# A rearranged opening, an identity made by GpSimd, and earlier loads and transposes of k in a fused attention and gated-MLP kernel

## The chip, the cores and the metric

The kernel runs on one core of one Trainium2 chip. The metric is the device time in microseconds (us) from launch to end; the median of three runs of the kernel before is 317.84 us (317.53 to 318.85). Beside these, one execution was recorded by the hardware profiler. Its time is 318.65 us, its span from the first to the last recorded instruction 316.9 us. Durations in this text come from that execution.

The engines are called as the profile calls them: PE (TensorE, matrix multiply; its weight loads are PEld), DVE (VectorE), ACT (ScalarE), POOL (GpSimd) and SP (SyncE, here only a queue that issues DMAs). Each engine works through its own instruction stream in order, and waits on semaphores for the others.

## What is computed

Sliding-window causal attention, followed by a feed-forward block with the gate h cos(h):

```python
# q, k, v: (batch 8, heads 8, seq 576, head_dim 64)
scores = scale * np.matmul(q, k.transpose(0, 1, 3, 2))
rel = pos[:, None] - pos[None, :]
mask = (rel >= 0) & (rel < 64)
scores = np.where(mask, scores, -1000000000.0)
attn = np.exp(scores - np.max(scores, axis=-1, keepdims=True))
attn = attn / (np.sum(attn, axis=-1, keepdims=True) + 1e-09)
attn_out = np.matmul(attn, v)
x = attn_out.transpose(0, 2, 1, 3).reshape(4608, 512)
h = x @ w_in            # 512 x 2048
g = h * np.cos(h)
out = g @ w_out         # 2048 x 512
```

Inputs and output are float32.

## The kernel before

**Tiling.** Tokens of all batches form one row of 4608, cut into nine tiles (`mt`) of 512. A batch has 576 tokens, nine blocks (`j`) of 64, so that batch borders and tile borders drift apart. Heads are taken in four pairs (`p`). A score *unit* is one block of 64 queries of both heads of a pair against its 128 keys, a 128x128 tile. Up to four units make a *group*, which has one PSUM bank. Groups 0 to 7 (written `p.g` in the list, half tile g of pair p) hold the blocks of tile 0; groups 8 to 18 hold the last block of batch 0 and all of batch 1; later ones hold a batch each.

**A group's way.** `g_scores` (PE; for groups 0 to 7 an extra matmul with the identity adds the mask, L267), `g_max` (DVE, L293 or L297), `g_exp` (ACT, L308, one exp for each unit), `g_inv` (DVE, L315), `g_norm` (L322, mostly on POOL), `g_trans` (on PE for the first groups and some others, L331, followed by `g_put`; otherwise a DMA transpose from SP's queue, L334, tile wT), `values` (PE, L349 or L368 for half tiles), `put_x` (copies to xT).

**The feed-forward part.** For a tile, 16 groups of matmuls with w_in (L418, or L382 in half tiles) each fill a bank; ACT makes the sine (cos(h) as sin(h + pi/2)), DVE multiplies (L543, or L394 in half tiles), which frees the bank. Then 64 matmuls with w_out (L551, or L401 for tile 0), and a copy to `out_sb`, of which there are two buffers; `store` sends each from SP's queue (L433). ACT's exp and sine use different function tables, and a change of table costs a load.

**Loads.** POOL's queue issues all loads: `load_heads` (q and k of batches 0 and 1, one head pair at a time, L162), `load_chunk` (later batches, six chunks of 96 tokens, L169), `load_v` (five chunks, L175), the four parts of w_in and of w_out (L191, L194). `spread_v` (L180 to L188) makes a copy of v shifted by a half block; for batches from 3 on it is two copies on POOL. q is transposed on PE. k is transposed on PE for batches 0 and 1, and from batch 2 on by six DMA transposes from SP's queue (`turn_k`, L239), into one of two buffers kT.

**What sets the order.** The opening (tile 0, and the attention of batch 1) is written out as a list, `FIRST`, one word a step; each step issues its instructions on its engine, so the list's order is each engine's order. Words: `Lq0.p`, `Lk0.p`, `Lq1.p` and so on are loads; `ms` clears qB (DVE, 0.54 us each); `io` is `put_steps`, `id` `put_ident`, `mk` `put_masks`, `mc` `cast_masks`; `tq.p`, `tk.p` (batch 0) and `Tq.p`, `Tk.p` (batch 1) are transposes on PE, `pq`, `pk`, `Pq`, `Pk` the copies out of PSUM with the engine behind the last dot (d for DVE, a for ACT, p for POOL, s for SP); `s`, `m`, `e`, `i`, `n`, `w`, `c` are a group's steps in the order given above, `c` being `g_put`; `v` and `x` are `values_half` and its copy; `h`, `S`, `g` are a half tile's first product, sine and gate (`h.g.f.bank`); `zA`, `zB`, `zC` and `y` are pieces of `spread_v`; `tb`, `tb2` load the sine and the exp table; `Gs` to `Gp` are the steps of groups 8 to 18; `V`, `X` are values and copies of tile 1; `o.part.m.bank` and `oc` are the second product of tile 0 and its copies. The last number of `s`, `h`, `o` and `Gs` picks one of five PSUM banks. Another three PSUM buffers are shared in turn by the transposes and the value matmuls.

From tile 1 on, one loop issues PE's matmuls, and between them `pump` issues what a plan (`at(time, ...)`) has due. Planned times are in units of about 1 us; a tile takes T = 32. For batch b, t0 = 32 (b - 1): the stage in which its scores are taken is tile b - 1's, from t0 + 14.6 on. On one engine or queue, a step with an earlier planned time stands ahead of one with a later.

## Time and profile before

| stretch (us from the span's start) | PE busy | DVE busy | ACT busy | POOL busy |
|---|---|---|---|---|
| 0 to 4.56 (4.56) | 0.00 | 3.14 | 1.49 | 3.45 |
| 4.56 to 8 (3.44) | 2.68 | 1.69 | 1.66 | 2.57 |
| 8 to 12 (4.00) | 3.98 | 2.68 | 2.90 | 3.56 |
| 12 to 18 (6.00) | 5.53 | 5.51 | 5.18 | 5.28 |
| 18 to 20 (2.00) | 1.27 | 1.54 | 2.00 | 1.91 |
| 20 to 24 (4.00) | 3.88 | 3.94 | 4.00 | 3.52 |
| 24 to 26 (2.00) | 1.97 | 1.77 | 1.98 | 0.77 |
| 26 to 30 (4.00) | 2.93 | 3.93 | 3.05 | 4.00 |
| 30 to 40.75 (10.75) | 10.75 | 10.25 | 7.43 | 6.59 |
| 40.75 to 62 (21.25) | 20.70 | 16.82 | 18.58 | 18.60 |
| 62 to 70 (8.00) | 8.00 | 6.48 | 6.39 | 8.00 |
| 70 to 96 (26.00) | 25.33 | 20.73 | 22.10 | 14.04 |
| 96 to 160 (64.00) | 63.99 | 52.80 | 54.00 | 51.50 |
| 160 to 192 (32.00) | 31.08 | 24.74 | 25.43 | 24.19 |
| 192 to 285 (93.00) | 93.00 | 68.44 | 65.48 | 44.41 |
| 285 to 317 (32.00) | 27.90 | 12.43 | 10.77 | 0.00 |

The profiled execution took 318.65 us, its span is 316.9 us. The table sets the busy time of each engine beside the length of a stretch: where PE's number falls short of the length, PE stood still. The opening runs until about 60, tile 1's stage starts at 60.6, tile 2's at 94.0, then one about every 32 us (126.2, 158.5, 191.7, 223.9); after 285 only the feed-forward part of the last tile is left. Loads of 144 KB in the opening took 5.8 us from issue to landing in the median, those of 96 KB (a chunk of q or k of a later batch) 8.9, a store of 512 KB 8.2.

### The profile page before, as it was taken

The page shows a single profiled execution, that of the slowest core. Times are in us where ns is not written, and L with a number is a line of the kernel's source. Part 1 is how long each engine was busy: PE and PEld are TensorE (multiplying, and loading weights), DVE is VectorE, ACT ScalarE, POOL GpSimd, SP SyncE. Part 2 cuts the span into 40 slices and gives each one's busy share as a digit, 9 for nine tenths or more (in the row PEclk, how much of TensorE's full clock was granted, in tenths as well). Part 3 has the DMA queues.
Part 4 walks back from the last instruction along what each step waited for, and adds up shares of the span by engine and source line. Part 5 has one row for each costly group of instructions (what it writes and reads, how often), then busy time and mean ns, then how long its engine had stood idle before and what let it go on. Part 6 is the DMA issues. An engine that isn't in the chain of part 4 may idle for free.

```text
span 316.9 us, 7926 instructions
## 1 busy us (share of the span) xinstructions
PE 303.0 (96%) x2635; PEld 161.2 (51%) x2635; DVE 236.9 (75%) x888; ACT 232.4 (73%) x777; POOL 192.4 (61%) x226
## 2 busy tenths in 40 slices
...
GB/s 91 182 200 160 189 182 161 132 167 160 214 79 135 145 218 75 114 120 229 91 112 140 232 102 95 161 208 135 93 160 100 86 130 63 0 68 66 1 66 66
DMA packets 154873, 40.60 MB, mean 128 GB/s; under 512 B 143248, under 2 KB 150352, under 8 KB 154832
## 3 DMA queue, kind: packets, MB, share of 16 engines
...
q8 instruction: 20, 0.33, 0.5%
...
q10 hardware_dynamic: 144, 0.13, 0.1%
HBM read 36.70 MB, written 9.44 MB: 146 GB/s over the span
## 4 chain that ended last, share of the span: by engine, by line
PE 63%; DVE 13%; ACT 9%; DMA 8%; POOL 4%; issue 3%; SPq 0%; POOLq 0%; DVEq 0%; ACTq 0%
PE out_ps L551 24%; PE h_ps L418 23%; ACT e L308 7%; DVE gT L543 6%; DMA q<-in_q_dram 4%; PE h_ps L382 4%; PE out_ps L401 4%; PE o_ps L349 3%; DMA out_dram<-out_sb 2%; POOL w L322 2%; PE s_ps L277 2%; DVE qB L128 2%; DVE s L297 2%; DMA wT<-w 1%; PE s_ps L283 1%
## 5 line engine op out<-in xcount | busy, mean ns | idle before, releaser
L551 PE MATMUL out_ps<-w_out,gT 128*128 128x512 bf16 x512 | 121.0, 379 | 0.0
L418 PE MATMUL h_ps<-xT,w_in 128*128 128x512 bf16 x512 | 116.2, 379 | 0.8 <-DVE gT L543 0.4
L540 ACT ACTIVATE sin<-h_ps 128x512 f32<-128x512 f32 x128 | 74.2, 598 | 37.8 <-PE h_ps L418 35.7
L308 ACT ACTIVATE e<-s,negm 128x128 f32<-128x128 f32 x256 | 98.7, 389 | 1.9 <-DVE negm L297 1.9
L543 DVE TENSOR_TENSOR gT<-h_ps,sin 128x512 bf16<-128x512 f32 x128 | 81.5, 686 | 21.4 <-ACT sin L540 20.7
L322 POOL TENSOR_TENSOR w<-e,rden 128x512 bf16<-128x512 f32 (+1 forms) x75 | 71.4, 962 | 40.4 <-DVE rden L315 31.1
L418 PEld LDWEIGHTS <-w_in 128*128 128x128 bf16 x512 | 48.2, 98 | 54.7 <-issue 1.0
L551 PEld LDWEIGHTS <-gT 128*128 128x128 bf16 x512 | 47.2, 98 | 46.1
L297 DVE CUSTOM_DVE_ANT_0 s<-s_ps,mask 128x128 f32<-128x128 f32 x256 | 58.5, 286 | 1.7 <-PE s_ps L283 1.0
L308 ACT ACTIVATION_READ_ACCUMULATOR e<-s,negm 128x1 f32 x256 | 48.4, 189 | 0.0
L169 POOL DMA_DIRECT2D q<-in_q_dram x36 | 29.2, 811 | 9.5 <-DMA q<-in_q_dram 4.1
L175 POOL DMA_DIRECT2D v<-in_v_dram x40 | 34.1, 871 | 0.2
L169 POOL DMA_DIRECT2D k<-in_k_dram x36 | 28.9, 805 | 5.6 <-DMA k<-in_k_dram 3.8
L315 DVE RECIPROCAL rden<-den 128x4 f32<-128x4 f32 (+1 forms) x79 | 13.7, 174 | 21.6 <-ACT e L308 20.8
L128 DVE COPY out_sb<-out_ps 128x512 f32<-128x512 f32 (+1 forms) x19 | 12.9, 676 | 19.6 <-PE out_ps L551 12.5
L128 ACT COPY out_sb<-out_ps 128x512 f32<-128x512 f32 x17 | 9.8, 575 | 21.7 <-PE out_ps L551 20.7
L277 PEld LDWEIGHTS <-qB 128*128 128x128 bf16 x216 | 17.0, 98 | 15.3 <-DVE negm L297 1.4
L128 DVE CAST xT<-o_ps 128x512 bf16<-128x512 f32 x31 | 20.1, 680 | 5.2 <-PE o_ps L349 5.1
L277 PE MATMUL s_ps<-kT,qB 128*128 128x128 bf16 x216 | 21.9, 219 | 0.9 <-DVE negm L297 0.9
L128 DVE COPY qB<-tq_ps 64x576 bf16<-64x576 bf16 x48 | 21.6, 451 | 0.3
L297 DVE DVE_READ_ACCUMULATOR2_ANT negm<- 128x1 f32 x256 | 21.4, 84 | 0.0
L128 POOL COPY v<-v 64x1536 bf16<-64x1536 bf16 (+1 forms) x10 | 16.8, 1682 | 5.3 <-DMA v<-in_v_dram 5.0
...
## 6 DMA issues: line engine op xcount, KB each, us to landing
...
```

Source lines behind the costliest of these rows:

```text
L128: {"a": nc.scalar.copy, "p": nc.gpsimd.tensor_copy}.get(engine, nc.vector.tensor_copy)(out, in_)
L169: nc.gpsimd.dma_start(out=st[name, b][:, c].rearrange("p (h d) -> p h d", h=H), in_=src.rearrange("h p d -> p h d"))
L175: nc.gpsimd.dma_start(out=vt.rearrange("p (h d) -> p h d", h=H), in_=v[b, :, c * 128:c * 128 + n, :].rearrange("h p d -> p h d"))
L277: nc.tensor.matmul(out=s_ps[:, u].rearrange("p (a t) -> p a t", a=2), lhsT=qblocks[(b % 2) * PAIRS + p][:, j].rearrange("d h t -> d (h t)" ...
L297: nc.vector.tensor_tensor_reduce(out=s[:, u], in0=s_ps[:, u], in1=mask[:, 2 - j % 2 if j else 0], scale=-scale if b else -1.0, scalar=BIG, ...
L308: nc.scalar.activation(e[:, u], s[:, u], AF.Exp, bias=negm[:, u:u + 1], scale=1.0 if n < n_first else -1.0, accum_out=den[:, u:u + 1])
L315: nc.vector.reciprocal(out=rden[:, 0:len(groups[n])], in_=den[:, 0:len(groups[n])])
L322: (nc.gpsimd if engine == "p" else nc.vector).tensor_tensor(out=w[:, 0:u], in0=e[:, 0:u], op=ALU.mult, in1=rden[:, 0:u].unsqueeze(2).to_br ...
L418: nc.tensor.matmul(out=st["h", ff], lhsT=w_in_sb[:, ks, ff * 128:ff * 128 + 128], rhs=st["xT", mt][:, ks], start=start, stop=stop)
L540: nc.scalar.activation(sin, h_ps, AF.Sin, bias=math.pi / 2.0)
L543: nc.vector.tensor_tensor(out=gt[:, e], in0=h_ps, in1=sin, op=ALU.mult)
L551: nc.tensor.matmul(out=o_ps[e], lhsT=gT[ff // 2][:, ff % 2, ms * 128:ms * 128 + 128], rhs=w_out_sb[:, ff], start=ff == 0, stop=ff == n_ff - 1)
```

## The change

There are two parts.

**The opening.** The list is replaced by one in another order. Several steps also change their engine or bank: for instance pk.0 goes from ACT to DVE and pq.0 from DVE to ACT, Pq.0 and Pq.1 from DVE to ACT, x.0.0 and x.1.0 from ACT to DVE, c.2.1 and c.3.1 from DVE to ACT, Gn.15 from DVE to POOL. The step `id` is gone: the identity is made by `make_identity`, which issues two instructions on POOL at the program's start, ahead of the first load:

```python
nc.gpsimd.memset(identity, 0.0)
nc.gpsimd.affine_select(out=identity, in_=identity, compare_op=ALU.not_equal,
                        fill=1.0, base=0, pattern=[[-1, 128]], channel_multiplier=1)
```

`put_steps` was one iota of 192 columns, from which DVE made the identity and, by two rescalings of half the partitions each, the distances for the masks. Now two iotas (64 partitions by 128 columns each) write these distances directly, and DVE begins with the squares.

**Later stages.** The loads of a batch's k and q were interleaved, chunk by chunk; now all of k goes first, and for batches from 4 on it goes to the start of the stage (t0 - 31.5 on), while q follows at t0 - 22.7 on. v's loads for batches from 4 on move from t0 + 0.5 to t0 + 5.3. `turn_k` for batches from 4 on moves from t0 - 5.5 to t0 - 26. For batch 3 only the order of k and q changes; batch 2 stays.

```diff
--- before.py
+++ after.py
@@ -44,27 +44,27 @@
 
 
 FIRST = (
-    "ms.0.d Lq0.0 Lk0.0 ms.1.d ms.2.d io id tq.0 mk Lq0.1 mc pq.0.d Lk0.1 tk.0 pk.0.a s.0.0.0 Lq0.2 tq.1 "
-    "tk.1 m.0.0 pq.1.a ms.3.d s.0.1.1 Lk0.2 tq.2 pk.1.d s.1.0.2 Lq0.3 Lk0.3 tk.2 s.1.1.3 e.0.0 tq.3 "
-    "m.0.1 Lq1.0 Lk1.0 Lq1.1 pq.2.d pk.2.d Lk1.1 tk.3 m.1.0 s.2.0.4 Lv0.0 Lv0.1 Tq.0 Lv0.2 pk.3.d m.2.0 "
-    "e.0.1 pq.3.a i.0.0 e.1.0 Tk.0 s.3.0.0 Tq.1 e.2.0 Lwi.0 Pq.0.d i.1.0 Lwi.1 m.3.0 Lv0.3 m.1.1 i.2.0 "
-    "Pk.0.a e.3.0 Lwi.2 Tk.1 n.1.0.p s.2.1.1 Pq.1.d Gs.10.2 m.2.1 Gs.9.4 n.0.0.p Pk.1.a n.2.0.p i.3.0 "
-    "e.1.1 w.0.0 zA.0.d w.1.0 c.0.0.d Gs.12.0 w.2.0 n.3.0.p i.0.1 c.1.0.d zA.1.d c.2.0.d e.2.1 n.0.1.p "
-    "i.1.1 w.3.0 v.0.0 c.3.0.d x.0.0.a s.3.1.3 Gm.10 v.1.0 m.3.1 i.2.1 Gs.11.2 Gm.9 Gm.12 n.1.1.p "
-    "x.1.0.a zB.1.d e.3.1 ms.4.d w.0.1 w.1.1 c.1.1.a i.3.1 h.0.0.1 h.0.1.4 tb n.2.1.p c.0.1.d Lwi.3 "
-    "w.2.1 h.0.2.0 zB.0.d n.3.1.p v.0.1 S.0.0 Gm.11 w.3.1 S.0.1 h.0.3.3 Lwo.0 S.0.2 c.2.1.d c.3.1.d "
-    "v.1.1 zC.s g.0.0 S.0.3 h.0.4.2 ms.5.d x.0.1.a x.1.1.d h.0.5.1 g.0.1 h.1.0.4 g.0.2 g.0.3 S.0.4 "
-    "ms.6.d h.0.6.0 h.1.1.3 S.0.5 S.1.0 Lq1.2 S.0.6 g.0.4 S.1.1 g.1.0 h.1.2.2 Lk1.2 ms.7.d Lq1.3 h.0.7.4 "
-    "g.0.5 h.1.3.1 Lv1.0 Lwo.1 g.1.1 S.1.2 h.1.4.3 g.0.6 Lk1.3 S.0.7 h.1.5.0 g.1.2 h.1.6.2 Lwo.2 g.0.7 "
-    "S.1.3 S.1.4 S.1.5 Lwo.3 h.1.7.4 Lv1.1 S.1.6 g.1.3 g.1.4 S.1.7 g.1.5 Lv1.2 g.1.6 tb2 Tk.2 Lv1.3 "
-    "Pk.2.d Ge.10 Tq.2 Pq.2.d Tq.3 Ge.9 Ge.12 o.0.0.1 Pq.3.d Tk.3 o.1.0 Pk.3.d Lq2.0 Ge.11 Gs.14.3 Gi.10 "
-    "Gm.14 g.1.7 Lq2.1 Gs.13.0 Lq2.2 o.0.1.2 Gi.9 o.2.0 Ge.14 Gn.10.p Lq2.3 Gm.13 Gc.10 Gi.12 Gs.8.3 "
-    "o.1.1 Gs.16.4 Gm.8 o.3.0 Ge.13 o.2.1 Gs.15.0 Gi.11 oc.0.d Gn.9.p o.3.1 Gn.12.p o.0.2.3 Gi.14 Gm.15 "
-    "Gs.17.1 Lq2.4 oc.1.d Gc.9 Gn.11.p Gi.13 Lq2.5 Gm.16 o.1.2 Ge.8 Ge.16 Ge.15 y.1.d Gn.14.p Gi.8 Gc.12 "
-    "Lv0.4 Gm.17 o.0.3.0 Gi.16 Gn.13.p Gc.11 Gn.8.p o.2.2 Gn.16.d Gw.8 y.0.s Gc.14 Gc.13 Lk2.0 Gp.8.d "
-    "o.3.2 Gi.15 Gw.16 Lk2.1 Ge.17 Lk2.2 o.1.3 Gn.15.d V.1 Gp.16.d oc.2.a Gw.15 Gi.17 Lk2.3 o.2.3 V.0 "
-    "Gp.15.d X.1.a Gn.17.d X.0.d V.2 V.3 X.2.a X.3.d Gc.17 o.3.3 oc.3.a Gs.18.2 Gm.18 Ge.18 Lk2.4 Gi.18 "
-    "Gn.18.d Gc.18 Lk2.5 Lv1.4 "
+    "ms.0.d ms.1.d Lq0.0 Lk0.0 ms.2.d tq.0 Lq0.1 io mk Lk0.1 Lq0.2 ms.3.d Lk0.2 Lq0.3 Lk0.3 tk.0 mc "
+    "Lq1.0 pk.0.d pq.0.a s.0.0.0 m.0.0 s.0.1.1 tq.1 Lk1.0 tk.1 e.0.0 Lv0.0 Lq1.1 Lwi.0 m.0.1 pq.1.d "
+    "pk.1.d Lv0.1 tq.2 Lk1.1 tk.2 s.1.0.2 tq.3 i.0.0 pq.2.a pk.2.d e.0.1 n.0.0.p pq.3.a tk.3 m.1.0 "
+    "s.2.0.3 e.1.0 pk.3.d s.1.1.4 m.2.0 i.0.1 w.0.0 s.3.0.0 Tq.0 m.1.1 Lwi.1 Tk.0 m.3.0 i.1.0 zA.1.d "
+    "e.2.0 i.2.0 s.2.1.1 m.2.1 Lv0.2 Lv0.3 s.3.1.2 e.3.0 n.1.0.p c.0.0.d n.2.0.p Pq.0.a i.3.0 m.3.1 "
+    "zA.0.d w.1.0 Pk.0.a w.2.0 n.3.0.p Lwi.2 Gs.9.3 w.3.0 c.1.0.d c.2.0.d n.0.1.p v.0.0 e.1.1 Gs.10.0 "
+    "c.3.0.d e.2.1 x.0.0.d v.1.0 Tq.1 x.1.0.d e.3.1 i.1.1 ms.4.d Lwi.3 Gm.10 n.1.1.p Gm.9 i.2.1 Tk.1 "
+    "Pq.1.a i.3.1 h.0.0.4 Lwo.0 h.0.1.1 Pk.1.d tb h.0.2.0 S.0.0 n.3.1.d zC.s w.1.1 S.0.1 n.2.1.p h.0.3.2 "
+    "w.0.1 c.1.1.d zB.1.d w.3.1 S.0.2 w.2.1 h.0.4.3 c.2.1.a ms.5.d g.0.0 zB.0.d c.0.1.d h.0.5.4 v.0.1 "
+    "c.3.1.a Lwo.1 g.0.1 g.0.2 S.0.3 v.1.1 ms.6.d S.0.4 ms.7.d h.0.6.1 g.0.3 g.0.4 x.0.1.a x.1.1.a Lq1.2 "
+    "Lv1.0 h.0.7.0 S.0.5 h.1.0.2 S.0.6 g.0.5 S.0.7 Lk1.2 S.1.0 g.0.6 h.1.1.3 S.1.1 g.0.7 Lq1.3 g.1.0 "
+    "h.1.2.4 S.1.2 h.1.3.1 Lv1.1 g.1.1 S.1.3 Lk1.3 g.1.2 g.1.3 h.1.4.0 h.1.5.2 S.1.4 h.1.6.3 Lv1.2 "
+    "h.1.7.4 g.1.4 S.1.5 g.1.5 Tk.2 S.1.6 g.1.6 Lv1.3 Gs.12.1 Tq.2 Lwo.2 Lwo.3 y.0.s S.1.7 Gs.11.0 tb2 "
+    "Pk.2.d Ge.10 Gm.12 Tq.3 Pq.2.d y.1.s Gs.8.2 Tk.3 Lq2.0 Gm.11 Ge.9 Gi.10 o.0.0.3 Lq2.1 g.1.7 Gs.14.1 "
+    "o.1.0 Lq2.2 Lq2.3 Pk.3.d Lq2.4 Gs.13.0 Lq2.5 Gn.10.p Ge.11 Gi.9 Gm.14 Ge.12 o.0.1.4 Pq.3.d o.2.0 "
+    "Lk2.0 Ge.14 Gi.11 o.1.1 Gm.13 Gs.16.1 Ge.13 o.2.1 Gi.12 Gm.8 Gs.15.0 Gc.10 Gi.14 o.3.0 o.3.1 Gm.16 "
+    "Ge.16 Gn.9.p o.0.2.2 oc.0.d Gi.13 Gc.9 Gs.17.1 oc.1.d Ge.8 Gs.18.3 Gn.11.p Gn.12.p Lk2.1 Gn.14.p "
+    "Gm.15 Lk2.2 Gi.16 Gc.11 o.0.3.4 Gm.17 Gn.13.p Gi.8 Gn.16.d o.1.2 Ge.15 Lk2.3 Lv0.4 Lk2.4 Lk2.5 "
+    "o.1.3 Gc.12 Gn.8.d Gc.14 Gi.15 o.2.2 Gw.8 Gm.18 Ge.17 Gw.16 Gp.8.d Ge.18 Gn.15.p Gi.17 Gn.17.p "
+    "o.3.2 Gc.13 Gw.15 Gp.16.d V.1 Gc.17 Gp.15.a oc.2.d o.2.3 Gi.18 V.0 X.1.d V.2 X.2.a V.3 Gn.18.p "
+    "o.3.3 X.0.d oc.3.a Gc.18 Lv1.4 X.3.d "
 )
 
 
@@ -130,18 +130,12 @@
 
 
     def put_steps():
-        nc.gpsimd.iota(mask.rearrange("p u c -> p (u c)")[:, 0:192], pattern=[[1, 192]], base=0, channel_multiplier=-1,
-                       allow_small_or_imprecise_dtypes=True)
-
-    def put_ident():
-        nc.vector.tensor_scalar(ident, mask[:, 0], 0.0, 1.0, ALU.is_equal, ALU.mult)
+        for h in range(2):
+            nc.gpsimd.iota(mask[64 * h:64 * h + 64, 0], pattern=[[2, 128]], base=-65, channel_multiplier=-2,
+                           allow_small_or_imprecise_dtypes=True)
 
     def put_masks():
-        steps = mask.rearrange("p u c -> p (u c)")
-        for h in range(2):
-            nc.vector.tensor_scalar(mask[64 * h:64 * h + 64, 2], steps[64 * h:64 * h + 64, 64 * h:64 * h + 128],
-                                    2.0, -65.0, ALU.mult, ALU.add)
-        nc.vector.tensor_tensor(out=mask[:, 2], in0=mask[:, 2], in1=mask[:, 2], op=ALU.mult)
+        nc.vector.tensor_tensor(out=mask[:, 2], in0=mask[:, 0], in1=mask[:, 0], op=ALU.mult)
         nc.vector.tensor_scalar(mask[:, 1], mask[:, 2], 64.0 ** 2, NEG, ALU.is_gt, ALU.mult)
         nc.vector.tensor_scalar(mask[:, 2], mask[:, 1], -1.0, NEG, ALU.mult, ALU.add)
         nc.vector.tensor_copy(mask[:, 0, 0:64], mask[:, 2, 0:64])
@@ -468,13 +462,13 @@
             for lag, fn, *args in ((0, tr_q), (0.02, put_block, 0), (0.5, put_block, 1)):
                 at(t_q + lag, fn, b, p, *args)
         if b > 2:
-            for c in range(NC):
-                for i, name in enumerate(("q", "k")):
-                    at(t0 - T + 5.6 + 1.6 * c + 0.8 * i, load_chunk, name, b, c)
+            for i, name in enumerate(("k", "q")):
+                for c in range(NC):
+                    at(t0 - T + (5.6 + 4.8 * i if b == 3 else 0.5 + 8.8 * i) + 0.8 * c, load_chunk, name, b, c)
         for c in range(NC):
-            at(t0 + (2 + 1.2 * c if b == 2 else c - 5.5), turn_k, b, c)
+            at(t0 + (2 + 1.2 * c if b == 2 else c - 5.5 if b == 3 else 1.1 * c - 26), turn_k, b, c)
         for c in range(5):
-            at(t0 + 0.5 + c, load_v, b, c)
+            at(t0 + (0.5 + c if b < 4 else 5.3 + 0.8 * c), load_v, b, c)
         for half_ in range(2):
             at(t0 + (14.45 + 0.1 * half_ if b > 2 else 10), spread_v, b, half_, "p" if b > 2 else "s")
     for mt in range(2, n_mt):
@@ -485,6 +479,7 @@
             at(time + 0.3 + 0.2 * (p % 2), put_x, mt, p)
 
 
+    make_identity(nc, ident)
     nc.vector.memset(small, 0.0)
     exp_table()
 
@@ -499,7 +494,7 @@
              "Lv0": lambda c: load_v(0, c), "Lv1": lambda c: load_v(1, c), "Lq2": lambda c: load_chunk("q", 2, c), "Lk2": lambda c: load_chunk("k", 2, c),
              "Lwi": lambda i: load_w_in(i * d_ff // W_PARTS, (i + 1) * d_ff // W_PARTS),
              "Lwo": lambda i: load_w_out(i * n_ff // W_PARTS, (i + 1) * n_ff // W_PARTS),
-             "io": put_steps, "id": put_ident, "mk": put_masks, "mc": cast_masks, "ms": clear_first,
+             "io": put_steps, "mk": put_masks, "mc": cast_masks, "ms": clear_first,
              "tq": lambda p: tr_q(0, p), "tk": lambda p: tr_k(0, p), "Tq": lambda p: tr_q(1, p), "Tk": lambda p: tr_k(1, p),
              "pq": lambda p, engine: put_q(0, p, engine), "pk": lambda p, engine: put_k(0, p, engine),
              "Pq": lambda p, engine: put_q(1, p, engine), "Pk": lambda p, engine: put_k(1, p, engine),
```

## The prediction

> **What bounds the kernel now.** I read the page's head first, then the list of who waited for whom on PE, then the timeline of the opening by engine, then stage 4, the only later one with a long PE wait.
>
> ```profile
> PE 303.0 (96%) x2635; PEld 161.2 (51%) x2635; DVE 236.9 (75%) x888; ACT 232.4 (73%) x777; POOL 192.4 (61%) x226
> ```
> ```profile
> PE tq_ps L203 <- DVE mask L146: 4.6, 1, 4.6
> PE s_ps L283 <- ACT kT L128: 1.4, 3, 0.7
> PE o_ps L368 <- DVE v L128: 1.1, 1, 1.1
> PE s_ps L277 <- DVE negm L297: 0.9, 1, 0.9
> PE tq_ps L203 <- DMA q<-in_q_dram: 0.6, 1, 0.6
> PE h_ps L418 <- DVE gT L543: 0.4, 1, 0.4
> PE h_ps L418 <- ACT out_sb L128: 0.3, 1, 0.3
> ```
> TensorE is busy for 303.0 of 316.9 us, and the order of its work is all that can be won: 4.6 us lie before the first transpose, 3.6 after the last matmul (it ends at 313.3), some 5.6 between. The first wait is charged to the masks, but DVE had made the identity by 3.2; what came last is the first q load (issued at 1.25, below; the transposes start at 4.56). The rest of the waits are four short ones in the opening, two around the turn from the opening into tile 1 (0.3 at 60.6, 0.4 at 75.5), one in stage 4. No stage is bound by another engine for long, so a gain is at most the 5.6 plus what the start allows.
>
> ```profile
> 1.25 0.74 POOL L162 DMA_DIRECT2D q<-in_q_dram  x1 [0.80 <-POOLq L578]
> ...
> 2.60 0.34 POOL L133 IOTA mask<- 128x192 f32 x1
> ```
> ```profile
> 23.89 0.56 ACT L308 ACTIVATE e<-s_ps,negm 128x128 f32<-128x128 f32 x1
> ...
> 24.09 0.61 DVE L128 COPY v<-v 64x1024 bf16<-64x1024 bf16 x1
> ...
> 25.84 1.18 DVE L128 COPY v<-v 64x1024 bf16<-64x1024 bf16 x1
> ...
> 27.07 0.44 PE L368 MATMUL o_ps<-wT,v 128*64 128x64 bf16 x16 [1.10 <-DVE v L128]
> ...
> 28.46 0.67 DVE L394 TENSOR_TENSOR gT<-h_ps,sin 128x512 bf16<-128x512 f32 x1
> ```
> The opening is a relay: ACT's exps (one starts 0.345 after another) until the last at 23.89, then DVE's backlog (two v spreads, copies, memsets) until the first gate at 28.46, which alone frees the bank of the sixth half-tile matmul h.0.5 (PE takes it up at 29.02). From there to 39.76 PE runs through.
>
> **Identity and masks.** Gone: the identity on DVE (0.23), two rescalings (two starts 0.31 apart, 0.59 in all). Added on POOL: a memset and a select of 128x128 ahead of the very first load, and a second iota, both after Lq0.1. No row has the select. Lower bound 0: POOL sits 0.80 idle before that load, and DVE's first memset shows engines free at 0.81, so 0.44 may hide both. Upper bound 0.67, two operations as long as the iota's 0.335. I take 0.30, between them (a memset's row is 0.10, a select should be near the iota; part hides). The first transposes go from 4.56 to 4.86. The iotas (0.25 each, from the 0.34 of 192 columns) end at 4.0, the masks at 5.15 (their five remaining operations took 1.11), ACT's casts at 6.2, then qT by ACT (0.65) and kT by DVE (0.76) at 7.0: the first scores' start goes from 6.67 to 7.05. **Loss 0.4 there**, with 0.1 to 0.8 as ends.
>
> **The list, walked with rows of this trace.** ACT: e.0.0 now stands ahead of a pair's copy, 8.4 instead of 9.14; then ACT waits for tq.2 (PE: s.0.1 to 8.75, three transposes of 0.67, 10.7), copies it, and starts e.0.1 at 11.4 (11.15 before). Then no gap: pq.3 0.65, e.1.0 13.45, e.2.0 14.85, e.3.0 16.25 (17.44 before: a 0.82 wait and Pk.0's 0.53 stood ahead). n.3.0 on POOL, fourth of four but no longer behind two loads of w_in, ends at 19.2 (20.18). c.3.0, v.1.0, x.1.0 by DVE: 20.0, 20.65, 21.3; h.0.0 starts at 21.35 against 22.92. ACT goes on with two copies, three exps groups of 1.4 and Pq.1: sine table at 23.5 (25.03), first sine 24.9 (26.43).
> DVE decides what follows. Between x.1.0 (21.3) and g.0.0 stand i.1.1 0.10, ms.4 0.57, Gm.10 and Gm.9 0.85 each (taken as full groups), two i 0.20, Pk.1 0.75, n.3.1 0.69, c.1.1 0.40, zB.1 0.61, ms.5 0.54: 5.56. So g.0.0 runs 26.9 to 27.5 and h.0.5 starts at 27.55 (PE waits 0.85). zB.1 is the loose one: the same copy took 0.61 beside loads being issued and 1.18 while POOL ran a norm (25.71 to 26.74). In the new list n.2.1 should be done at 24.9, before it; the other end adds 0.57. [...]
> From h.0.5: eleven half-tile groups of 0.87, two value groups of 0.37, waits of 0.15 (c.0.1) and 0.5 (g.0.3 behind two memsets): 10.95, so PE is through at 38.5 against 39.76. But Gs.11 and Gs.12, done before 29 in the old list, now come after: 0.51 (fourteen score matmuls at 43.14). **Gain 0.75**, from -0.7 (both loose ends against it, one more wait of DVE's length) to 1.6.
> Every load of the opening is issued in another order, too. Lwi.2 is the only one that goes far back, behind n.3.0: issued at 19.2 instead of 14.77, it has 6.6 us until h.0.4 (25.8); Lwi.3 took 5.0 from 23.68 to its landing. Covered; without that cover, up to 2 us.
>
> **The turn into tile 1.**
> ```profile
> 60.61 3.03 PE L418 MATMUL h_ps<-xT,w_in 128*128 128x512 bf16 x12 [0.33 <-ACT out_sb L128]
> ```
> In the old list score group 18 is last: its exps hold ACT from 60.72 to 62.3, the sine table until 63.7, so tile 1's gates run late and PE waits again 0.41 at 75.45. In the new list Gs.18 stands before o.0.3. ACT then has 40 exps of 0.385 from 40.6 to 56.0, before PE is through the second product (59.5 by the walk), and the sine table follows oc.3 directly. **Gain 0.33 + 0.41 = 0.74**, ends 0 and 0.9; if Gn.15 (1.03 on POOL, was 0.69 on DVE) made V.3 late, the first 0.33 would stay.
>
> **Later stages.**
> ```profile
> 173.60 1.04 SPq L433 DMA_DIRECT2D out_dram<-out_sb  x2
> ```
> ```profile
> 180.93 0.69 DVE L128 COPY out_sb<-out_ps 128x512 f32<-128x512 f32 x1 [2.54 <-DMA out_dram<-out_sb]
> ...
> 182.58 0.40 PE L277 MATMUL s_ps<-kT,qB 128*128 128x128 bf16 x4 [0.92 <-DVE negm L297]
> ```
> SP's queue in stage 4 (from 158.5) first works off wT transposes mixed with six of kT, 1.2 to 1.3 each, so both stores leave at 173.6, 15 us late; their landing at 180.9 frees out_sb, DVE stands 2.54, PE 0.92. The change moves six kT transposes (for b of 4 and more) from 5.5 before a stage to 6 after the start of the stage before. Some 7.8 us go from in front of the stores, which then leave some 8 us earlier. **Gain 0.92**, ends 0 and 1.2. Moved past on POOL: six k loads go ahead of five v loads, these ahead of six q loads; 17 issues as before. v's last issue moves from about 5 to about 10 us after the stage's start, ahead of the spreads at about 18. On SP a kT transpose waits for its k load (median 8.9 to landing), with nothing due behind it until the wT at about 20. Batch 3's transposes stay, so the 0.3 wait at 93.6 does too.
>
> **Sum.** 0.75 + 0.74 + 0.92 = 2.41: span 316.9 to 314.5. The profiled run took 318.65, 0.81 above the median 317.84, so part of what I read (I suspect the 0.92, which hangs on DMA timing) may be missing from the median. All of it off the median gives 315.4, without the 0.92 316.35. I forecast **316.0**; its own range is 315.0 to 316.9.
>
> **Rivals.**
> *The opening gives back what it gains* (0.25): g.0.0 comes no earlier than 28.5, because DVE loses zB's 0.57 and half a microsecond elsewhere, or the start costs 0.8. For it: DVE is the bound from 21 on. Against it: 1.5 us of lead on ACT. Then only 0.5 to 0.9 of the turn and stage 4 remain: 317.1.
> *PE's clock comes up at another time* (0.10). Eighteen transposes start 0.67 apart in sets until 11.76, 0.28 at 12.98.
> ```profile
> 11.76 0.69 PE L203 MATMUL tk_ps<-ident,k 64*64 64x64 bf16 x18
> ...
> 12.98 0.45 PE L203 MATMUL tq_ps<-ident,q 64*64 64x64 bf16 x18
> ```
> PE now waits less between 7 and 12; if the fast rate comes before tq.1, tq.2 is done 0.8 earlier and the whole ACT relay with it: 315.2 (0.06). If it comes three microseconds later, two exps groups slip by about 1.2: 317.2 (0.04). [...]
> *Slower: v lands late* (0.15). Place: the two v spreads on POOL, ahead of all norms of stages 3 to 6. In stage 3 the norms began 23.0 after the stage's start (149.2) with no PE wait in that stage; that is the point from which it decides. Now v goes out behind k: 0.9 + 4.6 + 4.3, some 2 of queue waits, then its landing; 5.0 (POOL waited so long at 234, behind nothing) makes 16.8, harmless; 8.9, as k and q take in the crowd, makes 20.7, plus 3.4 of spreads 24.1. Each stage then loses 1.1, in four 4.4, and gains 1.5 in the opening: 320.7. Against it: kT's transposes no longer crowd the stage's head.
> *The forecast* holds 0.50.
>
> **How the numbers follow.** Half a percent (1.6 us) is about what a measurement can tell from no change. Of the forecast's 0.50, 0.40 lies below 316.25 and 0.10 above; with the early clock (0.06) faster is 0.46. Same: 0.10 + 0.25 + 0.04 = 0.39; slower 0.15. The range 314.4 to 318.8 takes in the upper end of the terms (1.6 + 0.9 + 1.2 is 3.7, 314.1) nearly whole, the rival that gives back with the start's 0.8 on top, and leaves out most of the late v.
>
> **What would show it.** First transposes near 4.9; e.3.0 near 16.3; first gate before 28; PE through the half tiles at 38.5; no wait at 60.6 and 75.5; both stores in stage 4 gone within 10 us of its start and no 0.9 at negm. Wrong if g.0.0 is no earlier, or if POOL stands at v's spreads in stages 3 to 6.

## The result: 323.34 us, 1.2% slower, and the profile after

The changed kernel takes 323.34 us in the median of four runs (319.96 to 323.94). The kernel before took 318.17 us in the runs beside them (317.53 to 318.85). The ratio is 1.0124, with a 95% interval of 1.0082 to 1.0167: slower. This ratio and those below are estimated from the single executions, without any that is over 1.5% above the fastest of its kernel, and are not quotients of the medians (here 1.016). The profiled execution took 323.85 us, its span is 322.1 us, against 316.9 before: 5.2 us to be found.

The head of the page, and the list of who waited for whom on PE (waited for: us in total, times, longest):

```profile
PE 300.7 (93%) x2593; PEld 162.5 (50%) x2635; DVE 234.8 (73%) x883; ACT 232.4 (72%) x777; POOL 193.6 (60%) x230
```
```profile
PE tq_ps L197 <- DMA q<-in_q_dram: 4.9, 1, 4.9
PE o_ps L343 <- DMA wT<-w: 3.3, 6, 1.3
PE h_ps L376 <- issue: 2.3, 1, 2.3
PE o_ps L343 <- DMA v<-in_v_dram: 2.2, 1, 2.2
```

The 0.9 at negm and the two waits at the turn into tile 1 are gone, as forecast. In their place stand three that were not there: 3.3 for DMA transposes of w, 2.3 for "issue" in the first half-tile product, 2.2 for a load of v. The span by stages (a stage begins with the tile's first matmul with w_in) says where they fall. 32.14 is a full stage without any wait; tile 2's stage is the one from 94.0 before and from 95.75 after.

| us | opening, to tile 1's start | tile 1 | tile 2 | tile 3 | tile 4 | tile 5 | tiles 6, 7 |
|---|---|---|---|---|---|---|---|
| before | 60.61 | 33.42 | 32.14 | 32.33 | 33.23 | 32.14 | 61.24 |
| after | 63.46 | 32.29 | 34.11 | 32.71 | 33.81 | 32.75 | 61.24 |
| difference | +2.85 | -1.13 | +1.97 | +0.38 | +0.58 | +0.61 | 0 |

**The opening until 40** did nearly what the walk said. POOL's timeline (start, length, line, operation, tiles):

```profile
0.74 0.20 POOL masks.py:197 MEMSET ident<- 128x128 bf16 x1 [0.29 <-POOLq L573]
1.02 0.29 POOL masks.py:199 TENSOR_SCALAR_AFFINE_SELECT ident<-ident 128x128 bf16<-128x128 bf16 x1
1.44 0.74 POOL L156 DMA_DIRECT2D q<-in_q_dram  x1
...
3.23 0.58 POOL L134 IOTA mask<- 64x128 f32 x2
```

The identity puts off the first load by 0.19 (1.25 before); the first transposes start at 4.90, the first scores at 7.13. The first half-tile product starts at 20.96, and stops after one matmul (PE's timeline; in brackets the idle time before, and what ended it):

```profile
20.96 0.28 PE L376 MATMUL h_ps<-xT,w_in 128*128 128x256 bf16 x1
23.52 2.68 PE L376 MATMUL h_ps<-xT,w_in 128*128 128x256 bf16 x23 [2.27 <-issue]
```

"issue" means that the profile shows no semaphore and no engine that ended this wait. In the same stretch a DMA queue called "instruction" (q8), which carries 20 pieces of 16 KB in the whole span, carries one, from 21.22 to 22.31. In the trace of before a piece runs from 18.52 to 19.41, and the list of PE's waits has none for "issue". I took the piece for PE's own instructions, come late; that is a guess, since no view shows what a piece holds or who waits for it. What repeats is the place: in every profile that has this wait, PE stops behind the first matmul of h.0.0.

**The end of the opening.** The chain of work that ended last (start, length, what), between 51 and 59, then the windows of the next stretch (busy time of PE, PEld, DVE, ACT, POOL with the number of instructions; PEclk; DMA share; GB/s):

```profile
51.00 1.05 POOL w L316
52.06 0.74 POOL k L163
52.80 6.07 DMA v<-in_v_dram
58.86 0.04 issue
58.91 0.47 PE o_ps L343 x16
59.37 1.82 PE out_ps L395 x4
```
```profile
56.70:58.90 2.20, 0.00 (x0) 0.00 (x0) 0.66 (x2) 0.95 (x5) 1.74 (x3) 1.00 2.41 153
59.30:62.60 3.30, 3.30 (x57) 1.85 (x54) 1.39 (x2) 0.36 (x1) 3.30 (x4) 0.50 1.76 85
```

In the kernel before, POOL's load and PE's V.1 stood at:

```profile
50.43 0.73 POOL L175 DMA_DIRECT2D v<-in_v_dram  x1
```
```profile
56.45 0.44 PE L349 MATMUL o_ps<-wT,v 128*64 128x64 bf16 x16
```

V.1, the first value product of tile 1, needs Lv0.4, the last chunk of batch 0's v. POOL issues it at 52.80 (50.43 before), because in the new list Lk2.0 to Lk2.3 stand ahead of it; it lands at 58.86. PE stands still for 2.24, and then runs 3.4 us at a granted clock of 0.50: four matmuls with w_out take 1.82 instead of 1.04. In this profile that is 2.24 plus 1.7 (half of 3.4), the whole of the opening's loss and more.

**Tile 2's stage.** SP's queue, and PE at the end of the stage:

```profile
106.88 2.31 SPq L427 DMA_DIRECT2D out_dram<-out_sb  x2
109.32 9.89 SPq L233 DMA_TRANSPOSE kT<-k  x6
119.31 8.69 SPq L328 DMA_TRANSPOSE wT<-w  x6
```
```profile
124.63 0.28 PE L343 MATMUL o_ps<-wT,v 128*64 128x64 bf16 x6 [1.28 <-DMA wT<-w]
125.24 0.51 PE L343 MATMUL o_ps<-wT,v 128*64 128x64 bf16 x20 [0.33 <-DMA wT<-w]
```

Before, the queue had stood empty between the stores and wT:

```profile
104.39 2.16 SPq L433 DMA_DIRECT2D out_dram<-out_sb  x2
114.37 10.46 SPq L334 DMA_TRANSPOSE wT<-w  x7
```

Until 106.8 SP works off the transposes of batch 3's k, which come late as before. Then, behind two stores, it takes the six of batch 4, which now come early. The wT transposes, which had begun at 114.37, 20.3 after the stage's start, with the queue empty for 7.8 us ahead of them, begin at 119.31, 23.6 after it.

**Tiles 3 to 5.** The stores leave early now (at 168.27 in stage 4, 5.7 after its start; 15 before), and the 0.92 is won. But POOL's queue, here in tile 3's stage from 129.86 on, shows the rival that I had called "v lands late":

```profile
129.00 4.62 POOL L163 DMA_DIRECT2D k<-in_k_dram  x6
133.61 4.24 POOL L169 DMA_DIRECT2D v<-in_v_dram  x5
...
145.16 1.59 POOL L163 DMA_DIRECT2D q<-in_q_dram  x2 [3.42 <-DMA v<-in_v_dram]
147.79 0.77 POOL L163 DMA_DIRECT2D q<-in_q_dram  x1 [1.05 <-DMA v<-in_v_dram]
149.82 3.41 POOL L128 COPY v<-v 64x1536 bf16<-64x1536 bf16 x2 [1.25 <-DMA v<-in_v_dram]
153.31 3.03 POOL L316 TENSOR_TENSOR w<-e,rden 128x512 bf16<-128x512 f32 x3
```

The norms (start of the last row, less 129.86) begin 23.5 after the stage's start; in the next two stages 24.3 and 23.5 (23.0, 21.1 and 19.3 before). v's chunks take 11.7 us to land in this stage (6.1 before). Norms past 23 make the wT transposes late, and PE waits for these 0.38 at 158.1, 0.82 at 191.7, 0.34 at 224.7.

### The profile page after: what moved, and what is told of

Its sections match the earlier page's. It is cut to its first block, busy times and chain, and to the rows that moved or that the text cites. A ratio compares the mean times of both kernels' runs of the same rounds, so it can differ in the third digit from the quotient of the medians.

```text
span 322.1 us, 7876 instructions
## 1 busy us (share of the span) xinstructions
PE 300.7 (93%) x2593; PEld 162.5 (50%) x2635; DVE 234.8 (73%) x883; ACT 232.4 (72%) x777; POOL 193.6 (60%) x230
## 4 chain that ended last, share of the span: by engine, by line
PE 52%; DVE 18%; DMA 12%; POOL 9%; issue 4%; ACT 3%; POOLq 0%; DVEq 0%
PE out_ps L546 20%; PE h_ps L412 19%; DVE gT L538 9%; DMA v<-in_v_dram 8%; POOL w L316 4%; DVE s L291 4%; PE h_ps L376 3%; PE out_ps L395 3%; DVE qB L128 3%; PE o_ps L343 3%; DMA wT<-w 3%; ACT e L302 3%; DMA k<-in_k_dram 2%; POOL v L128 2%; PE s_ps L271 1%
## 5 line engine op out<-in xcount | busy, mean ns | idle before, releaser
L546 PE MATMUL out_ps<-w_out,gT 128*128 128x512 bf16 x491 | 118.8, 379 | 1.2 <-issue 0.2
L163 POOL DMA_DIRECT2D q<-in_q_dram x36 | 28.0, 785 | 23.3 <-DMA v<-in_v_dram 20.3
L128 DVE CAST xT<-o_ps 128x512 bf16<-128x512 f32 x33 | 21.6, 683 | 12.8 <-PE o_ps L343 12.8
L163 POOL DMA_DIRECT2D k<-in_k_dram x36 | 28.1, 795 | 0.0
```

What stands on the lines that cost most here:

```text
L128: {"a": nc.scalar.copy, "p": nc.gpsimd.tensor_copy}.get(engine, nc.vector.tensor_copy)(out, in_)
L163: nc.gpsimd.dma_start(out=st[name, b][:, c].rearrange("p (h d) -> p h d", h=H), in_=src.rearrange("h p d -> p h d"))
L546: nc.tensor.matmul(out=o_ps[e], lhsT=gT[ff // 2][:, ff % 2, ms * 128:ms * 128 + 128], rhs=w_out_sb[:, ff], start=ff == 0, stop=ff == n_ff - 1)
```

## The experiments

The theory after reading the two traces: the opening loses by the place of one load, Lv0.4; the later stages lose by two things that act together, k's transposes early and v's loads behind k's. Its rivals: that the new list itself is slower, that the later stages lose only because the opening leaves them another phase, and that v's place alone, or the transposes' place alone, is the whole cause. Every ratio is against runs of the kernel before on the same chip.

| kernel | median us | ratio to before (95%) | tile 1 starts at | stages of tiles 1 to 5 in the profile |
|---|---|---|---|---|
| e1_after_again | 323.96 | 1.0127 (1.0067 to 1.0186) | 65.90 | 32.26, 33.61, 32.13, 33.02, 32.72 |
| e2_later_only | 322.98 | 1.0090 (1.0051 to 1.0129) | 61.19 | 33.12, 36.16, 32.14, 38.07, 32.14 |
| e3_opening_only | 319.76 | 1.0010 (0.9971 to 1.0049) | 64.33 | 32.26, then 32.14 each |
| e4_lv04_early | 321.14 | 1.0064 (1.0033 to 1.0094) | 63.98 | 32.28, 33.41, 32.14, 33.55, 33.28 |
| f1_swap_full | 322.65 | 1.0124 (1.0066 to 1.0181) | 63.90 | 32.27, 34.76, 32.14, 33.17, 32.14 |
| f2_swap_old_later | 318.37 | 0.9987 (0.9953 to 1.0022) | 63.30 | 32.27, 32.14, 32.63, 33.62, 32.14 |
| f3_swap_turn_late | 319.54 | 1.0001 (0.9955 to 1.0047) | - | - |
| f4_swap_v_first | 318.99 | 1.0001 (0.9967 to 1.0036) | 61.86 | 32.30, 34.15, 32.14, 32.14, 32.14 |
| g1_late_wi_v_first_turn5 | 321.96 | 1.0092 (1.0058 to 1.0126) | 65.42 | 32.27, 32.13, 34.64, 32.13, 32.14 |
| g2_late_wi | 318.72 | 0.9998 (0.9961 to 1.0035) | 62.38 | 32.43, then 32.14 each |
| g3_turn_late_again | 318.85 | 0.9986 (0.9957 to 1.0015) | 62.35 | 32.26, 32.14, 32.17, 33.19, 32.22 |
| g4_ident_later | 321.76 | 1.0096 (1.0064 to 1.0127) | 62.08 | 32.27, 32.14, 34.50, 32.14, 32.14 |

The median of the kernel before was 318.98 beside e1 to e4, 318.53 beside f1 to f4, 318.87 beside g1 to g4.

### The two halves apart

**e1** is the changed kernel as it is.

> The changed kernel unaltered, to see which of its long waits are steady. Theory A (the waits have fixed causes in the order of loads): tile 1's stage starts again at about 63.5 us, PE waits 2 us and more for a v load ahead of V.1 near 57 and loses another 1.6 to a halved clock behind it, and the stages of tiles 2 to 5 take about 34.1, 32.7, 33.8 and 32.8; time 322 to 324. The wait of 2.3 us in the first half-tile product at 21 is either there again (cause in the order) or gone (a matter of chance). Rival B (one execution's chance): at least one of the two long waits of the opening is gone and the time is 320 or less, as one of the four runs was.

323.96 us: the loss repeats. V.1 waits 3.98 for v, and behind it four matmuls with w_out take 1.85 (from 61.70) instead of 1.04; the granted clock of this execution is 0.993. The wait for "issue" at the first half-tile product is not there. The later waits for wT are smaller in this profile: 0.54 and 0.55 in tile 2's stage, 0.29 and 0.32 in those of tiles 4 and 5, none in tile 3's.

**e2** keeps the old list, the old identity and masks, and has the new times of the later stages:

```diff
 before.py, FIRST as before
-at(t0 - T + 5.6 + 1.6 * c + 0.8 * i, load_chunk, name, b, c)
+at(t0 - T + (5.6 + 4.8 * i if b == 3 else 0.5 + 8.8 * i) + 0.8 * c, load_chunk, name, b, c)
-at(t0 + (2 + 1.2 * c if b == 2 else c - 5.5), turn_k, b, c)
+at(t0 + (2 + 1.2 * c if b == 2 else c - 5.5 if b == 3 else 1.1 * c - 26), turn_k, b, c)
-at(t0 + 0.5 + c, load_v, b, c)
+at(t0 + (0.5 + c if b < 4 else 5.3 + 0.8 * c), load_v, b, c)
```

> The opening as before, only the later stages' loads and transposes as changed. Theory A: the later stages cost on their own, stages of tiles 2 to 5 together about 2.5 to 3.5 us longer than before's 129.8 (94.0 to 223.9), time 320 to 321.5. Rival: they only suffer from the late opening and are harmless behind the old one; then the 0.9 stall in stage 4 goes and the time is 316.5 to 317.5.

322.98 us, a ratio of 1.0090: most of the loss, without the new list, and more than theory A's 320 to 321.5. The old opening's two waits at the turn (0.33 and 0.41) are there again. The profiled execution was the longest of ten (327.6 us), so the 36.16 and 38.07 of the table are not typical: PE waits 1.52 and 0.59 for wT in tile 2's stage and 2.66 in tile 4's, and each time its matmuls are slower behind the wait: 15 with w_out take 4.93 (from 124.99), 14 take 5.54 (from 194.58), where 15 take 3.63 at 228.64. The granted clock of this execution is 0.984, which over 325.8 us comes to some 10 us at half the clock (an estimate).

**e3** is the converse: the new list, identity and masks, the old times of the later stages.

```diff
 after.py, FIRST as after
-at(t0 - T + (5.6 + 4.8 * i if b == 3 else 0.5 + 8.8 * i) + 0.8 * c, load_chunk, name, b, c)
+at(t0 - T + 5.6 + 1.6 * c + 0.8 * i, load_chunk, name, b, c)
 ... (turn_k and load_v likewise)
```

> The new opening, later stages as before. Theory A: the opening costs 2.9 us by the start of tile 1's stage (63.5 against 60.6), of which tile 1's stage gives back about 1; the rest as before: 319.3 to 320.5. Rival: the opening costs nothing that lasts, 317 to 318.5.

319.76 us, 1.0010: no difference that can be measured. Its stages from tile 2 on are 32.14 each; there is no wait of PE of over 0.2 us after 63.9. PE's timeline at V.1, and the windows of tiles 2 and 3:

```profile
55.23 0.39 PE L325 MATMUL tw_ps<-ident,w 128*128 128x128 bf16 x4
59.73 0.46 PE L343 MATMUL o_ps<-wT,v 128*64 128x64 bf16 x16 [4.11 <-DMA v<-in_v_dram]
```
```profile
96.59:128.73 32.14, 31.87 (x253) 16.66 (x253) 26.33 (x113) 27.01 (x94) 26.21 (x30) 1.00 1.41 144
128.73:160.87 32.14, 31.88 (x254) 16.66 (x253) 26.34 (x113) 27.00 (x94) 26.27 (x30) 1.00 1.48 141
```

PE was there at 55.6 and waited 4.11; behind that four matmuls with w_out take 1.71 (from 60.13) instead of 1.04, and the granted clock of this execution is 0.992. So the new list is not measurably slower by itself. Without the wait and the half clock behind it tile 1 would begin at 64.33 - 4.11 - 1.7 = 58.5 by this profile (an estimate, with the 1.7 of the changed kernel), some 2 us before the 60.61 of the old list, and that is given back at V.1. The ratios of e2 and e3 together make 1.010; both together (e1) made 1.0127.

### The load of v

**e4** issues Lv0.4 before all of batch 2's k:

```diff
-    "Lk2.0 Ge.14 Gi.11 o.1.1 ...
+    "Lv0.4 Lk2.0 Ge.14 Gi.11 o.1.1 ...
-    ... Ge.15 Lk2.3 Lv0.4 Lk2.4 Lk2.5 "
+    ... Ge.15 Lk2.3 Lk2.4 Lk2.5 "
```

> The changed kernel with one word moved: Lv0.4, the last chunk of batch 0's v, stands ahead of Lk2.0 instead of behind Lk2.3 (some 8 us earlier on POOL). Theory A: V.1 waits for this load alone; the wait of 2.2 us before V.1 and the half clock behind it (1.6) go, tile 1's stage starts at 59.5 to 60 and the time falls by 3 to 4 to about 319.5. Rival: V.1 waits for a DMA transpose or the shifted copy of batch 1's v; then nothing moves by more than 0.5.

321.14 us, 1.0064, short of the 319.5 expected; tile 1 starts at 63.98. The wait at V.1 is gone, but one more load now stands early in POOL's queue: POOL stands 2.65 for a load of w_out to land before it can go on, its norms come later, and PE waits 2.28 at Gw.15 (59.08); behind that four matmuls with w_out take 1.46 (from 59.78) instead of 1.04, with a granted clock of 0.995 in this execution. The wait had only moved on. So the next kernel keeps the number of loads ahead as it was.

**f1** exchanges the two loads, Lv0.4 and Lk2.0; f2, f3, f4, g1, g2, g3 and g4 all have this:

```diff
-    "Lk2.0 Ge.14 Gi.11 o.1.1 ...
+    "Lv0.4 Ge.14 Gi.11 o.1.1 ...
-    ... Ge.15 Lk2.3 Lv0.4 Lk2.4 Lk2.5 "
+    ... Ge.15 Lk2.3 Lk2.0 Lk2.4 Lk2.5 "
```

> The changed kernel with two words of the list exchanged: Lv0.4 takes the place of Lk2.0 and Lk2.0 that of Lv0.4, so that no other load changes its place. Theory A: V.1 waits for Lv0.4 only, and the run that moved it alone met the next wait because Lk2.0 then held POOL; here both go, tile 1's stage starts at 59.5 to 60.5, PE's clock stays up at 60, the later stages stay as slow as they were (tiles 2 to 5 about 132.5 to 133.5 together); time 319 to 320.5. Rival: POOL's queue is full anyway, something else waits there for 2 us, and the start stays at 63.

322.65 us, 1.0124, as slow as the changed kernel, where 319 to 320.5 was expected. No wait at V.1, none at Gw.15, but no gain in time either: in this profile the "issue" wait is back at the first half-tile product (2.48), and the clock is halved behind it: 0.50 from 25.2 to 30.9, 0.80 in the mean from 22.6 to 25.1. The 23 matmuls that took 2.68 in the changed kernel take 5.09 here.

```profile
22.39 0.28 PE L376 MATMUL h_ps<-xT,w_in 128*128 128x256 bf16 x1
25.16 5.09 PE L376 MATMUL h_ps<-xT,w_in 128*128 128x256 bf16 x23 [2.48 <-issue]
```

The later stages lose as in the changed kernel (tile 2's 2.62 above 32.14, tile 4's 1.03).

### The later stages taken apart

**f2** is f1 with the old later stages (the edit of e3).

> The new opening with that exchange, and the later stages' loads and transposes as before the change. Theory A: both of the change's losses are gone; tile 1 starts at about 60, the stages of tiles 2 to 5 take 128.6 to 129.8 together; time 315 to 317, faster than before. Rival: the opening gains nothing once its wait is gone (start 60.6 or later), time 317 to 318.5.

318.37 us, 0.9987: the rival's time, not theory A's 315 to 317. Against f1, measured beside it, that is 4.3 us for the later stages. In the profiled execution (320.83, the longest of its ten) the "issue" wait stood at 2.38, the 23 matmuls behind it took 5.09 again, with a granted clock of 0.989 as in f1's, and stage 4 had the negm wait of before (1.31) back.

**f3** is f1 with the loads in the changed order but every kT transpose at its old time:

```diff
-at(t0 + (2 + 1.2 * c if b == 2 else c - 5.5 if b == 3 else 1.1 * c - 26), turn_k, b, c)
+at(t0 + (2 + 1.2 * c if b == 2 else c - 5.5), turn_k, b, c)
```

> As the exchange alone, but the DMA transposes of k stand where they stood before the change, while the loads keep the changed order (k first, v behind k, q last). Theory A (the early transposes crowd the loads): v's loads land in 6 to 8 us instead of 11.7 in the stage of tile 3, POOL waits little ahead of the spreads, the stages take 32.1 to 32.5; time 315 to 317. Rival B (v behind k is what makes it late): the norms still start 23 us and more after the stage's start, and the stages take 32.5 to 34 as in the changed kernel.

319.54 us, 1.0001. The profiled execution of this one took 1095.94 us with PE's matmuls several times longer from end to end (those with w_in 1.10 us in the mean against 0.38 in the changed kernel), and can't be read; so the same kernel was taken once more as g3.

> The run with the transposes of k where they were and the changed order of loads, once more, since its profile fell on an execution with PE at a quarter of its speed throughout. Theory A (transposes crowd the loads): v's loads land in 6 to 8 us, stages 32.1 to 32.5. Rival B (v behind k): norms of tiles 3 to 5 start 23 us and more after their stage's start and stages take 32.5 to 34. The runs of the order with v in front speak for B in tiles 3 to 5 and for A in tile 2's stage; so I now expect tile 2's stage at 32.1 and one or two of the others at 32.5 to 33.5.

318.85 us, 0.9986. v's loads still stand behind k's and take 8.5 us to land in tile 3's stage, between the 6.1 of before and the 11.7 of the changed kernel:

```profile
v<-in_v_dram POOLq DMA_DIRECT2D x4, 128.0 KB, 8.5
```

The norms of that stage begin 22.5 after its start (149.29, with the stage from 126.75): short of 23, and there is no wait for wT in any stage. What is left of the later loss is the 0.88 at negm in stage 4, where the stores leave late again (14.4 after its start). So v behind k alone costs nothing that shows in the time.

**f4** is f1 with the transposes early, and v's loads for batches from 4 on ahead of k's:

```diff
-at(t0 + (0.5 + c if b < 4 else 5.3 + 0.8 * c), load_v, b, c)
+at(t0 + (0.5 + c if b < 4 else 0.1 + 0.05 * c), load_v, b, c)
```

> As the exchange alone, but v's loads go ahead of k's at the start of a stage; the transposes of k stay early. Theory A (transposes): the spreads are in time, since v lands early, but q's loads still land late and hold POOL, so the norms still start late; stages of tiles 2 to 5 hardly shorter than 132.5. Rival B (v behind k): the norms start by 20 to 21 us after the stage's start, no wait for wT of over 0.3, the stages take 32.1 to 32.4; time 315.5 to 317.

318.99 us, 1.0001, against 1.0124 for f1, but not the 315.5 to 317 of rival B. POOL's timeline in tile 3's stage (from 128.31):

```profile
127.41 4.26 POOL L169 DMA_DIRECT2D v<-in_v_dram  x5
131.62 4.65 POOL L163 DMA_DIRECT2D k<-in_k_dram  x6
136.19 0.84 POOL L163 DMA_DIRECT2D q<-in_q_dram  x1
...
143.38 3.43 POOL L128 COPY v<-v 64x1536 bf16<-64x1536 bf16 x2
147.44 1.03 POOL L316 TENSOR_TENSOR w<-e,rden 128x512 bf16<-128x512 f32 x1 [0.64 <-POOL v L128]
```

The DMA view of the same stage (KB each, median us from issue to landing) has v at 5.0, against 11.7 in the changed kernel:

```profile
v<-in_v_dram POOLq DMA_DIRECT2D x4, 128.0 KB, 5.0
```

The norms begin 19.1 after the stage's start instead of 23.5, the stages of tiles 3, 4 and 5 are 32.14 each, and the 0.9 of stage 4 is won too. So the losses of tiles 3 to 5 need both parts: they are gone with v in front (f4), and gone with the transposes late (g3). The two are not quite taken apart, since k lands later behind v: in tile 3's stage of f4 k's loads go out from 131.62 on and land 8.1 later in the median, so that the transposes begin some 11 us after its start (an estimate from these two), when v has landed; in the changed kernel they begin 4.8 after it, beside v's loads. What remains in f4 is tile 2's stage, 34.15: it does not depend on v's place.

**g1** puts the border between late and early transposes one batch further, on top of f4 (and moves a load of the opening, below):

```diff
-at(t0 + (2 + 1.2 * c if b == 2 else c - 5.5 if b == 3 else 1.1 * c - 26), turn_k, b, c)
+at(t0 + (2 + 1.2 * c if b == 2 else c - 5.5 if b < 5 else 1.1 * c - 26), turn_k, b, c)
```

> The new opening with Lv0.4 and Lk2.0 exchanged and Lwi.1 moved behind n.3.0 (beside Lwi.2); in the later stages v's loads ahead of k's, and the early DMA transposes of k only from batch 5 on (batch 4 as before the change). Theory A for the opening (PE's own instruction fetch of 16 KB is queued behind Lwi.1's half megabyte): with no large load in the queue at 17 to 18.7 the fetch starts within 2 us of 17.5, no wait of over 1 us at the first half-tile product near 21, no halved clock after 13, tile 1 starts at 58 to 59. Rival: the wait has nothing to do with that load and comes as often as before (four of eight profiles), or Lwi.1 itself comes late and h.0.2 waits over 1 us for it. Theory A for the later stages: tile 2's stage was long because two batches' transposes of k stood in it, so now all stages take 32.1 to 32.4; time 313.5 to 315.5 where the opening holds. Rival: tile 2's stage stays at 33 and more.

The loss moves with the border. The windows of the stages of tiles 2 and 3, and SP's queue with PE's wait in the latter:

```profile
97.69:129.82 32.13, 32.13 (x257) 16.65 (x252) 25.92 (x113) 26.99 (x94) 26.05 (x30) 1.00 1.49 141
129.82:164.46 34.64, 32.52 (x259) 16.86 (x253) 26.50 (x113) 27.01 (x94) 28.07 (x32) 1.00 1.61 153
```
```profile
141.35 1.91 SPq L427 DMA_DIRECT2D out_dram<-out_sb  x2
143.37 9.71 SPq L233 DMA_TRANSPOSE kT<-k  x6
153.16 9.01 SPq L328 DMA_TRANSPOSE wT<-w  x6
```
```profile
159.56 0.78 PE L343 MATMUL o_ps<-wT,v 128*64 128x64 bf16 x24 [2.09 <-DMA wT<-w]
```

Tile 2's stage is free, tile 3's now holds two batches' transposes and takes 34.64, with 2.09 of waiting for wT. The stage in which late and early transposes meet pays; g4 (34.50, 1.92) shows it a second time. But g1 and g4 are about 0.9% slower than the kernel before; f4, whose stages of tiles 2 to 5 add up to nearly the same (130.57 against 131.04 and 130.92), is not, and neither is g2, which has the opening of g1. That part of their time is not explained.

### The opening: the wait for "issue" and the identity

Lwi.1 is a load of 512 KB that the new list issues before Lv0.2 and Lv0.3. In the changed kernel it landed at 21.21, and the piece on the instruction queue began at 21.22. Five profiles have the long wait (after, f1, f2, f4, g3); e1, e3 and e4, which have the same place for Lwi.1, do not. **g1**, **g2** and **g4** issue it behind n.3.0 instead:

```diff
-    ... s.3.0.0 Tq.0 m.1.1 Lwi.1 Tk.0 m.3.0 ...
+    ... s.3.0.0 Tq.0 m.1.1 Tk.0 m.3.0 ...
-    ... w.2.0 n.3.0.p Lwi.2 Gs.9.3 ...
+    ... w.2.0 n.3.0.p Lwi.1 Lwi.2 Gs.9.3 ...
```

g2 has beyond that only the exchange and the old later stages.

> The same opening, later stages as before the change. Opening as in the run with the later stages rearranged: theory A tile 1 at 58 to 59, rival 61 to 64. Later stages: 32.1 each but for one or two waits of about 1 us in tiles 3 and 4, which come and go from run to run. Time 314 to 316.5 by A.

g2 takes 318.72 us (0.9998), g1 321.96 (1.0092). Both are far from theory A (314 to 316.5, 313.5 to 315.5), and tile 1 starts at 62.38 and 65.42, in or past the rival's 61 to 64. The "issue" wait is 0.73 in g2, and in g1 and g4 there is none over 0.15; the granted clock of the profiled executions is 1.0 (g1, g4) and 0.999 (g2). With Lwi.1 where the changed kernel has it, the wait was 2.27 to 2.75 in five profiles and absent in three. With the old list (before, e2) there was none. So the wait came with the new list alone and varies from run to run; the place of Lwi.1 seems to bear on it, but three profiles against eight are few, and that the load holds up the piece is not shown: in the kernel before, Lwi.1 landed at 22.17, and a piece went from 18.52 to 19.41 all the same. The granted clock, which is on record for every execution, says more: one stretch of 3.41 us at half the clock takes it from 1 to 0.995, as in the changed kernel's profile. It was 0.998 or more in 7 of g2's 10 executions and in 3 of 10 of f2, which differs from g2 in Lwi.1 alone; and in none of the eight of the changed kernel, against 59 of the 82 of the kernel before that ran beside e1 to g4. Nothing was gained in time: w_in itself now comes late (waits of 0.38 and 0.52 in g2, 1.86 and 1.22 in g1), then Gw.15 (0.81, 1.35) and wT (1.60 in g2).

**g4** is g1 with the identity's two instructions issued behind Lk0.0 instead of ahead of the first load.

```diff
-    "ms.0.d ms.1.d Lq0.0 Lk0.0 ms.2.d tq.0 ...
+    "ms.0.d ms.1.d Lq0.0 Lk0.0 id ms.2.d tq.0 ...
```

> As the first kernel of this call, with the identity's two instructions on POOL moved behind Lk0.0. Theory: they cost about 0.3 us of start; the first transposes go from about 4.75 back to about 4.5 and everything behind by at most 0.3, less than a timing can show. Rival: nothing moves at the first transposes, because their start hangs on the load's transfer only.

321.76 us (1.0096) against g1's 1.0092. The first transposes start at 4.70 instead of 4.79; the other profiles with the identity in front have 4.72 to 4.94. So the identity ahead of the load costs a tenth or two at most, which the time does not show.

No version of the twelve beats the kernel before by more than its interval; f2 and g3 (0.9987 and 0.9986) come nearest. The theory that the opening loses by the place of Lv0.4 is borne out for the wait and not for the time. With the load back in front (f1, f2, f4, g1 to g4) no profile waits for v at V.1, but tile 1 never starts before 61.86, and the time does not fall: f1 has the ratio of the changed kernel, and f2 (0.9987) and e3 (1.0010), alike but for that load, have intervals that overlap. In its place came the wait for "issue", w_in, a norm or wT. What the times show is the cost of the later stages: 1.0090 alone in e2, and gone in f2, f3, g3 and f4.

## Why the prediction was wrong, step by step

**The start: right.** 4.86 and 7.05 were forecast, 4.90 and 7.13 came. The loss of 0.4 held. Not all of it is the identity's: the first load went out 0.19 later and the first transposes started 0.34 later, and in g4, where the first load goes out at 1.26 as in the kernel before, they still start at 4.70. Where the rest comes from is open.

**The list walked with rows: right, but for the wait for "issue".** h.0.0 was forecast at 21.35 and started at 20.96, the first sine at 24.9 and came at 24.49. The first gate came at 28.13 instead of 26.9, and PE was through the half tiles at 39.6 instead of 38.5, because PE stood 2.27 in h.0.0. In e1 and e3, which do not have this wait, the first gate is at 26.75 and 27.03 and PE is through at 38.25 and 38.53, as walked. The walk had no term for it: the rows of the kernel before show no such wait.

**"Lwi.2 is the only one that goes far back": wrong.** This sentence disposed of all loads of the opening. Lv0.4 goes back too, past four loads of k: POOL issued it 2.4 later, while PE was ready for V.1 as early as before (56.7 against 56.45) and, without the wait for "issue", earlier (55.6 in e3). In this profile it cost 2.24 of waiting (3.98 and 4.11 in e1 and e3), and the halved clock behind it another 1.7 (half of 3.4). Without these two, tile 1 would have begun at 63.46 - 2.24 - 1.7 = 59.5, just where the walk had put it; that is luck, since the wait for "issue" lies inside, and e3, which lacks it, comes to 58.5. That this time can be had is not shown: f1 to g4, which take the wait away, meet others instead. That the clock fell behind this wait, to 0.50 for 3.41 us, was in no term of the sum and in no rival; the rival on the clock looked only at its first rise. That moved as well: in e4 and g1, where a set of 18 transposes still took 0.67 at 12.77 and 13.05 and 0.45 only from 16.50 and 16.68 on (11.73 in the changed kernel), h.0.0 started at 22.92 and 23.09, in the other profiles with the new list at 20.96 to 22.39.

**The turn into tile 1: right, and too small.** 0.74 was forecast, 0.33 of it ahead of tile 1's first matmul and 0.41 within the stage. Both waits are gone, and the stage alone fell from 33.42 to 32.29, by 1.13: beside the 0.41, the wait of 0.26 for wT at 93.6 went, which the prediction had expected to stay, and the first twelve matmuls took 2.75 instead of 3.03. Every profile with the new list has 32.26 to 32.43 there, whatever its later stages.

**Later stages: the gain of 0.92 came, the loss was elsewhere.** The stores left 5.7 after the stage's start, and the wait at negm is gone in this as in every profile with early transposes. The suspicion that it comes and goes was right: of the five profiles whose later transposes are all late, before, f2 and g3 have it (0.92, 1.31, 0.88), e3 and g2 do not. Two sentences failed. "Batch 3's transposes stay, so the 0.3 wait at 93.6 does too" looked at batch 3 alone (and that wait went, in e2 as well): where its late transposes end, batch 4's early ones begin, and the 9.9 us of the latter put wT from 20.3 to 23.6 after the stage's start. That is 1.97 in the changed kernel, and 1.27 to 2.62 above 32.14 in every kernel with this border in tile 2's stage (e2's 4.02 has half clock in it). It was in no rival. The other is "On SP a kT transpose waits for its k load (median 8.9 to landing), with nothing due behind it until the wT at about 20": it weighed early transposes by what they stand ahead of in SP's queue, not by what they do to loads in flight. The runs show this in v's landing: 11.7, 12.5 and 9.4 us in the median in tiles 3 to 5 of the changed kernel, with v behind k and early transposes, 8.5 in tile 3's stage of g3, with v behind k and late ones.

**The rival "v lands late", given 0.15, came true in kind.** Its point of decision was norms past 23.0; they came 23.5, 24.3 and 23.5 after the stage's start, and these stages lost 0.57, 1.67 and 0.61 against 32.14 (1.1 each was its price, for four stages; tile 6's lost nothing). The point holds over the other profiles too: where norms began 23.2 or later in tiles 3 to 5, the stage was longer by 0.49 or more, and where they began by 22.5, with neither the wait at negm nor two batches' transposes in the stage, by 0.1 at most. It had taken 8.9 for v's landing, 11.7 was measured, and 24.1 for the norms. "kT's transposes no longer crowd the stage's head" stood against it as an argument, and was the reverse of what g3 shows: v behind k is harmless as long as the transposes are late. Its total, 320.7, lacked tile 2's stage and V.1.

In sum, by the one profile, forecast -2.4 on the span, measured +5.2: V.1 with its halved clock +3.9; the rest of the opening, where the walk's gain exceeds the wait for "issue", -1.1; tile 1's stage -1.1; tile 2's doubled transposes +2.0; tiles 3 to 5, with stage 4's 0.92 won within it, +1.6. The timed runs weigh the two halves otherwise: the new list alone is 0.1% slower (e3, -0.3 to 0.5), the new later stages alone 0.9% (e2, 0.5 to 1.3). The step that failed for the time is thus the later stages' "gain 0.92", which left out what the early transposes do to wT in tile 2's stage and to v's loads; in the opening, the forecast gain was taken by waits that the walk did not have.
